# Expert stage of a fused attention and mixture kernel: its buffers laid into the feed-forward's tiles, and its first gathers written earlier

## The chip, the cores and the metric

The kernel runs on one core of a Trainium2 chip. The metric is the device time of one execution in microseconds (us). Several executions are timed and their median is given; one further execution is recorded by the hardware profiler, and all rows below come from that one.

A core has a matrix engine (TensorE, PE in the rows; PEld is its loading of weights), a vector engine (VectorE, DVE), a scalar engine (ScalarE, ACT), a general engine (GpSimd, POOL) and SyncE (SP). Each works through a queue of its own in order and waits for the others by semaphores. SP and POOL also issue DMAs; PSUM is the memory into which TensorE writes.

## The reference

Three layers follow each other, on 2304 tokens of width 512:

```
attn = softmax(causal(q k^T / 8 + decay)) v       # 4 batches, 8 heads, 576 tokens
h    = attn @ w_in;  x = (h * clip(h + 3, 0, 6) / 6) @ w_out       # inner width 2048
e    = argmax(x @ w_gate)                          # one of 8 experts for each token
out  = prob(e) * sigmoid(x @ w_output_gate)[e] * (relu(x @ w1[e]) @ w2[e])   # inner width 1024
```

The change concerns the last layer, the expert stage, and the end of the layer in front of it.

## The kernel before

Numbers are kept as pairs of 16-bit values, a high part in f16 and a low part in bf16, so a product takes three matmuls (high x high, high x low, low x high). `P` is 128, `KD` is 4 (512 / 128), `E` is 8, `F2` is 1024, `CT` is 384.

The feed-forward runs over six chunks of 384 tokens (`moe1_steps`). Its weights lie in `wi` and `wo` in SBUF, its inner values in `g` (also seen as the flat `gf`; `wof` is the flat `wo`), its input chunks in two tiles with the tag `xT`. These tiles belong to pools `mp` and `mpi`, which the context `moe1_ctx` holds. `gate_steps` works out expert, rank and weight of each token and writes the chunk's result, row by row, into a DRAM tile `rows`.

An expert's tokens are found by their rank in it. `table` builds, by matmuls with one-hot tiles `R`, the token numbers (`ids`) and weights (`cf`) for slots of 128 tokens, called blocks: block 0, 1 and 2 of each expert. `gather` then issues for each block an indirect DMA from POOL, which fetches 128 rows of `rows` into `xg` (256 KB), and a transposing DMA from SP, which turns them into `xs`. `expert1` is the first product: 8 steps, each 12 matmuls into one PSUM tile, then a relu on ACT that writes the high part of `hT` and a subtraction on DVE that writes the low part. `expert2` is the second product, 24 matmuls for a block; ACT weighs the result into `y`, and an indirect DMA from POOL scatters it to the output.

Blocks 0 of experts 0 and 1 hold tokens of the chunks that are done first. They are gathered and computed early, around the last chunk's gating, with the lists `first` and a room in `wi` for everything. Then the expert stage proper (`round_`) goes through experts 0 to 7: first product of the main blocks (`main[e]`: block 1 for experts 0 and 1, blocks 0 and 1 for the others), block 2 under a branch that is taken only where the expert has more than 256 tokens (its two products are the third block), and the second product of the main blocks. In this data experts 0, 1, 4 and 6 take the branch.

The experts' weights come as f32, 512 KB at a time, by DMA from SP into a stage tile (`fetch` inside `weights_steps`), and are split into high part (ACT) and low part (DVE) in `W1` and `W2`, two tiles each. An expert has eight such parts. Experts 0 and 1 are split during the last chunk; `spread` hands out the other 48 splits between the steps of the products. Stage tiles are three in the pool `wp`, and four in the pool `xp` once `round_` starts. `xp` is opened behind the early blocks, after `moe1_ctx` is closed, and so takes the room of `wi`, `wo`, `g` and the chunks:

```
    moe1_ctx.close()
    xp = ctx.enter_context(tc.tile_pool(name="xp", bufs=1))
    stw_in[:] = xp, 4
```

`xg` has three tiles there, `xs` and `hT` two, `y` three. For TensorE, ACT and DVE the order in the expert stage is that in which the code is written (`manual_schedule`); for POOL and SP the scheduler sets it at build time.

Of the kernel before, what the change touches and what calls it, by code (L numbers as in the profile page):

```python
# [7 lines left out]
F16 = mybir.dt.float16  # L8
# [10 lines left out]
P = 128  # L19
# [39 lines left out]
def attention_moe_kernel(ctx: ExitStack, tc: tile.TileContext, q, k, v, f, w_in, w_out,  # L59
# [781 lines left out]

    stw_in, fetches = [], []

    def weights_steps(wp):

        parts, tiles = [], {}

        def add(e, which):  # L850
            wv = (w1, w2)[which][e].rearrange("(k p) f -> p k f", p=P)
            for i in range(KD):
                n = F2 // P // KD
                parts.append((wv[:, i] if which == 0 else wv[:, n * i:n * i + n], e, which,
                              i if which == 0 else slice(n * i, n * i + n)))

        for e, which in ((0, 0), (1, 0), (0, 1), (1, 1)):
            add(e, which)
        for e in range(2, E):
            add(e, 0)  # L860
            add(e, 1)
        sts = []

        def fetch():
            pool, bufs = stw_in
            st = pool.tile([P, F2], F32, tag="stw", name="stw", bufs=bufs)
            src = parts[len(sts)][0]
            if len(src.shape) == 3:
                st = st.rearrange("p (a b) -> p a b", a=src.shape[1])
            nc.sync.dma_start(out=st, in_=src)  # L870
            sts.append(st)

        for _ in range(3):
            fetch()
        fetches.append(fetch)
        yield
        for i, (_, e, which, js) in enumerate(parts):
# [68 lines left out]
    def gather(e, pool, blocks, into=None):  # L946

        n = len(blocks)
# [12 lines left out]
    def h_tile(e, blocks, into=None):  # L961
        n = len(blocks)
# [26 lines left out]
    def expert2(e, pool, ps_pool, blocks, into=None):  # L989

        W2 = wts[e, 1]
        NF2 = F2 // P
        for s in blocks:
            hT, ho = h_t[e, s]
            ps = ps_pool.tile([P, 512], F32, tag="mm", name="mm")
            i = 0
            for m in range(NF2):
                for a, b2 in ((0, 0), (0, 1), (1, 0)):
                    l, r = hT[:, m, a, ho:ho + P], W2[:, b2, m, :]
                    nc.tensor.matmul(ps, lhsT=l.bitcast(BF16) if a else l, rhs=r.bitcast(BF16) if b2 else r,  # L1000
                                     start=i == 0, stop=i == 3 * NF2 - 1)
# [71 lines left out]
    def open_weights():  # L1073
        nonlocal wp, wg_
        while adv():
            pass
        attn_ctx.close()
        wp = ctx.enter_context(tc.tile_pool(name="wp", bufs=1, side="right"))
        stw_in[:] = wp, 3
        wg_ = weights_steps(wp)  # L1080

    for c in range(NCH):
# [13 lines left out]
        for _ in moe1_steps(c):  # L1096
# [29 lines left out]
            if c == NCH - 1 and k_ > 8:  # L1126
                for i in [rq.pop(0) for _ in range(min(2, len(rq)))]:
                    rank_onehot(R0, i, 0, P)
                    rank_onehot(R, i, P, CAP)
                    if i == NBL - 1:  # L1130
                        reserve()
                        table(R0, 0, const, ps_mm, (0,), NBL)
                        for e in range(2):
                            row = wi[:, 0, 2 * e]
                            gather(e, None, (0,), (row[:, 0:2 * DM].rearrange("p (a b) -> p a b", b=P),
                                                   row[:, 2 * DM:4 * DM]))
                            h_tile(e, (0,), wi[:, 0, 2 * e + 1].rearrange("p (a c b) -> p a c b", c=2, b=P))
        if c < NCH - 1:
# [18 lines left out]
    run(first[0], 3)  # L1157
    run(first[1], 2)
    table(R, P, const, ps_mm, (1, 2), NB)
    for g_ in first:  # L1160
        run(g_, F2 // P)
    regs = []
    for e in range(2):
        for _ in expert2(e, None, ps_mm, (0,), wi[:, 1, e, 0:2 * DM].bitcast(F32)):
            pass
        if e == 0:
            regs.extend(nc.values_load(cnt[0:1, x:x + 1], min_val=0, max_val=NT) for x in range(E))  # L1167
            more = nc.values_load(nrounds[0:1, 0:1], min_val=0, max_val=NT // CAP)  # L1168
    moe1_ctx.close()
    xp = ctx.enter_context(tc.tile_pool(name="xp", bufs=1))  # L1170
    stw_in[:] = xp, 4

    def round_(first):
        main = [(1,) if first and e < 2 else (0, 1) for e in range(E)]

        def fetch(e):
            blocks = main[e] + (2,)
            gather(e, xp, blocks)
            h_tile(e, blocks)

        def when(e):

            return tc.If(regs[e] > CAP - P) if first else nullcontext()

        def spread(g, n):

            done = 0
            for i, _ in enumerate(g):
                if done < n and i % 2 == 0:
                    run(wg)  # L1190
                    done += 1
            run(wg, n - done)

        def first_product(e):
            spread(expert1(e, ps2, main[e]), KD if 0 < e < E - 1 else 0)
            with when(e):  # L1196
                for _ in expert1(e, ps_mm, (2,)):
                    pass
                for _ in expert2(e, xp, ps_mm, (2,)):
                    pass  # L1200

        wg = wg_
        if not first:
            wg = weights_steps(wp)
            run(wg, 4 * KD + 1)
        fetch(0)
        fetch(1)
        for _ in range(2 if first else 0):
            fetches[0]()
        for e in range(E):  # L1210
            first_product(e)
            if e + 2 < E:
                fetch(e + 2)
            spread(expert2(e, xp, ps2, main[e]), KD if e + 2 < E else 0)

    round_(True)
    manual.close()
    with tc.If(more > 0):
        RA = xp.tile([P, NB, CAP], F16, name="RA")
        with tc.For_i(0, more, 1):  # L1220
            nc.vector.tensor_scalar(out=rank, in0=rank, scalar1=-float(CAP), scalar2=None, op0=ALU.add)
            for i in range(NB):
                rank_onehot(RA, i, 0, CAP)
            table(RA, 0, xp, ps_mm, range(NSB), NB)
            round_(False)


# [28 lines left out]
```

## Time and profile before

| | us |
|---|---|
| median of 3 timed runs | 832.36 |
| lowest and highest of them | 831.86, 833.91 |
| the profiled execution | 829.8 |
| its span, first to last instruction | 828.1 |
| TensorE busy in the span | 738.6 (89%) |
| VectorE, ScalarE, GpSimd busy | 466.0, 450.5, 314.8 |

Attention and feed-forward overlap until about 550 us; the early blocks follow the last chunk at 581, and the expert stage fills the rest. Shares over the whole span say little about one stage, so stretches are read by windows and timelines. A time in a row is counted from the first instruction.

### The profile page before, as it was taken

How to read it: one execution, taken by the hardware profiler on the slowest of the kernel's cores; microseconds unless marked ns; L12 is line 12 of the kernel's file. 1: busy time of each engine (PE TensorE's matmuls, PEld its weight loads, DVE VectorE, ACT ScalarE, POOL GpSimd, SP SyncE). 2: the span in 40 equal slices, each digit the busy share in tenths (PEclk: the TensorE clock that was granted, in tenths of full speed). 3: DMA queues.
4: the chain of work that ended last, by engine and by line, in shares of the span. 5: the costliest groups of instructions: out<-in, count | busy, mean ns of one | idle time of the engine just before them, and what ended most of it. 6: DMA issues, size and time to landing. Idle time of an engine off the chain costs nothing. (4 is left out here: it accounts for less than half of the span.)

```text
span 828.1 us, 16598 instructions
## 1 busy us (share of the span) xinstructions
PE 738.6 (89%) x6177; PEld 477.7 (58%) x6177; DVE 466.0 (56%) x1267; ACT 450.5 (54%) x909; POOL 314.8 (38%) x393
## 2 busy tenths in 40 slices
PE   4756988988899999999999999999929899999994
PEld 2543555645566655566555656666707666756761
DVE  8998997547632855168515785740502566535410
ACT  4865789767973684479525665530203465535420
POOL 9557788755762453256413400000022132220010
PEclk9976989989999999999999999999969999999997
DMA  9767899979994783578515567420356599979010
GB/s 248 234 184 181 185 226 246 186 126 175 173 179 104 142 141 62 92 146 152 82 36 124 102 222 234 123 49 4 78 183 123 164 301 309 293 196 279 31 38 28
DMA packets 263778, 127.95 MB, mean 155 GB/s; under 512 B 214658, under 2 KB 247522, under 8 KB 263684
## 3 DMA queue, kind: packets, MB, share of 16 engines
q1 hardware_dynamic: 251860, 105.20, 57.8%
q0 software_dynamic: 4960, 15.73, 5.4%
q10 hardware_dynamic: 6864, 5.80, 2.6%
q8 instruction: 54, 0.88, 0.4%
q14 instruction: 40, 0.33, 0.1%
HBM read 71.52 MB, written 10.08 MB: 99 GB/s over the span
## 5 line engine op out<-in xcount | busy, mean ns | idle before, releaser
L695 PE MATMUL mm<-xT,wi 128*128 128x384 f16 (+1 forms) x1152 | 211.4, 331 | 7.9 <-DMA xT<-xn 5.2
L718 PE MATMUL mm<-g,wo 128*128 128x384 f16 (+1 forms) x1152 | 198.3, 326 | 1.5 <-DVE hr L702 1.4
L695 PEld LDWEIGHTS <-wi 128*128 128x128 f16 (+1 forms) x1152 | 111.2, 99 | 83.7 <-issue 15.6
L718 PEld LDWEIGHTS <-wo 128*128 128x128 f16 (+1 forms) x1152 | 111.0, 98 | 74.6 <-issue 3.6
L981 PEld LDWEIGHTS <-W 128*128 128x128 f16 (+1 forms) x1344 | 101.1, 99 | 28.2 <-issue 20.0
L981 PE MATMUL mm<-xs,W 128*128 128x256 f16 (+3 forms) x1152 | 98.2, 248 | 19.2 <-DMA xs<-xg 16.4
L884 DVE TENSOR_TENSOR W<-stw,W 128x1024 bf16<-128x1024 f32 x64 | 77.3, 1224 | 58.3 <-ACT W L883 57.7
L394 POOL TENSOR_TENSOR pn<-ms,pn 128x384 bf16<-128x384 f32 (+1 forms) x80 | 83.1, 1044 | 57.8 <-ACT pn L393 53.9
L376 ACT ACTIVATE ms<-ms,nm 128x512 f32<-128x512 f32 (+4 forms) x144 | 79.4, 576 | 37.6 <-DVE nm L342 26.4
L1000 PE MATMUL mm<-W,hT 128*128 128x512 f16 (+1 forms) x432 | 94.7, 379 | 1.1 <-ACT W L883 0.5
L883 ACT ACTIVATE W<-stw 128x1024 f16<-128x1024 f32 x64 | 66.3, 1052 | 21.6 <-DMA stw<-in_moe_w_dram 21.2
L985 DVE SCALAR_TENSOR_TENSOR hT<-mm,hT 128x128 bf16<-128x128 f32 (+1 forms) x96 | 33.0, 355 | 74.7 <-ACT hT L984 72.5
L342 DVE CUSTOM_DVE_ANT_1 ms<-sc,mask 128x128 f32<-128x128 f32 (+3 forms) x128 | 59.1, 485 | 24.8 <-PE sc L295 13.9
L707 DVE TENSOR_TENSOR g<-hr,g 128x384 bf16<-128x384 f32 x80 | 54.4, 682 | 31.2 <-ACT g L703 31.0
L1000 PEld LDWEIGHTS <-hT 128*128 128x128 f16 (+1 forms) x432 | 41.8, 98 | 51.3 <-ACT W L883 1.2
L702 DVE SCALAR_TENSOR_TENSOR hr<-hr,mm 128x384 f32<-128x384 f32 x96 | 52.7, 549 | 28.2 <-ACT hr L699 27.4
L699 ACT ACTIVATE hr<-mm,bias 128x384 f32<-128x384 f32 x96 | 54.5, 568 | 18.3 <-PE mm L695 16.2
L1007 POOL DMA_INDIRECT out_dram<-y,ids x18 | 18.7, 1038 | 119.0 <-ACT y L1006 102.4
L703 ACT ACTIVATE g<-hr 128x384 f16<-128x384 f32 x96 | 49.3, 516 | 26.4 <-DVE hr L702 25.8
L984 ACT ACTIVATE hT<-mm 128x128 f16<-128x128 f32 (+1 forms) x96 | 31.1, 331 | 53.9 <-PE mm L981 53.8
L428 PE MATMUL pv<-vt,pt 128*128 128x65 f16 x320 | 42.4, 199 | 17.0 <-DVE xs L453 8.6
L295 PE MATMUL sc<-K,q 128*128 128x256 f16 (+3 forms) x192 | 49.2, 297 | 7.0 <-DVE nm L342 6.8
(189 smaller groups left out, 1122.0 us busy)
## 6 DMA issues: line engine op xcount, KB each, us to landing
stw<-in_moe_w_dram SPq DMA_DIRECT2D x64, 512.0 KB
wo<-in_moe_w_in_dram SPq DMA_DIRECT2D x16, 512.0 KB
raw<-in_moe_w_out_dram ACTq DMA_DIRECT2D x11, 512.0 KB
rows<-rw POOLq DMA_DIRECT2D x15, 256.0 KB, 2.8
ldk<-in_k_dram SPq DMA_DIRECT2D x14, 256.0 KB
ldq<-in_q_dram SPq DMA_DIRECT2D x14, 256.0 KB
ldv<-in_v_dram SPq DMA_DIRECT2D x13, 256.0 KB
g<-in_moe_w_out_dram SPq DMA_DIRECT2D x3, 512.0 KB
```

The costliest lines, as they stand in the source:

```text
L342: nc.vector.tensor_tensor_reduce(out=pairs(ms[:, off:off + w]), in0=ps[:, 0:w].rearrange("p (c j) -> p c j", c=2), in1=pairs(mask[:, 640 - ...
L376: nc.scalar.activation(out=ms[:, off:off + w], in_=ms[:, off:off + w], func=AF.Exp, scale=-1.0, bias=nm[:, i:i + 1])
L394: nc.gpsimd.tensor_tensor(out=lo.bitcast(BF16), in0=ms[:, 0:N], in1=hi, op=ALU.subtract)
L695: nc.tensor.matmul(ps[:, 0:w], lhsT=l.bitcast(BF16) if a else l, rhs=r.bitcast(BF16) if b2 else r, start=i == 0, stop=i == 3 * KD - 1)
L699: nc.scalar.activation(out=hr, in_=ps[:, 0:w], func=AF.Relu, bias=bias3)
L702: nc.vector.scalar_tensor_tensor(out=hr, in0=hr, scalar=6.0, in1=ps[:, 0:w], op0=ALU.min, op1=ALU.mult)
L707: either.tensor_tensor(out=g[:, m, 1, 0:w].bitcast(BF16), in0=hr, in1=g[:, m, 0, 0:w], op=ALU.subtract)
L718: nc.tensor.matmul(ps[:, 0:w], lhsT=l.bitcast(BF16) if a else l, rhs=r.bitcast(BF16) if b2 else r, start=i == 0, stop=i == 3 * NF - 1)
L883: nc.scalar.activation(out=hi, in_=sts[i], func=AF.Copy)
L884: nc.vector.tensor_tensor(out=lo.bitcast(BF16), in0=sts[i], in1=hi, op=ALU.subtract)
L981: nc.tensor.matmul(ps[:, 0:w], lhsT=l.bitcast(BF16) if a else l, rhs=r.bitcast(BF16) if b2 else r, start=i == 0, stop=i == 3 * KD - 1)
L1000: nc.tensor.matmul(ps, lhsT=l.bitcast(BF16) if a else l, rhs=r.bitcast(BF16) if b2 else r, start=i == 0, stop=i == 3 * NF2 - 1)
```

## The change

Everything that lay in `xp` now lies in the feed-forward's own tiles, and `moe1_ctx` stays open: `xs` takes two rooms and `xg` six rooms in `g`, `hT` takes two rooms and `y` four rooms in `wo`. The rooms of `xg` and `y` are handed out by `row_tile`, whose one count `taken` serves both. Stage tiles are a ring of five: the three of `wp` and two of the chunks' `xT` tiles (named `stx`). Gathers of the first two experts, and two weight fetches, are written in front of the rest of the early blocks' code. `spread` takes the number of steps and gives expert 1's first product two splits instead of four, and expert 6's second product two instead of none.

```
-            st = pool.tile([P, F2], F32, tag="stw", name="stw", bufs=bufs)
+            if ring:
+                st = ring.pop(0)
+                ring.append(st)
+            else:
+                st = wp.tile([P, F2], F32, tag="stw", name="stw", bufs=3)
+                made.append(st)
...
+    taken = [0]
+
+    def row_tile(room):
+
+        i = taken[0] % (room.shape[1] // (2 * DM))
+        taken[0] += 1
+        return room[:, i * 2 * DM:(i + 1) * 2 * DM]
...
-            xs = pool.tile([P, 2 * KD, NSB * P], F16, tag="xs2", name="xs2", bufs=2)[:, :, 0:n * P]
-            xg = [pool.tile([P, 2 * DM], F16, tag="xg", name="xg", bufs=3) for _ in blocks]
+            n = 2 * KD * NSB * P
+            xs = gf[:, e % 2 * n:(e % 2 + 1) * n].rearrange("p (a b) -> p a b", a=2 * KD)
+            xg = [row_tile(gf[:, 2 * n:]) for _ in blocks]
...
-            into = xp.tile([P, F2 // P, 2, NSB * P], F16, tag="hT", name="hT", bufs=2)
+            n = F2 // P * 2 * NSB * P
+            into = wof[:, e % 2 * n:(e % 2 + 1) * n].rearrange("p (a c b) -> p a c b", c=2, b=NSB * P)
...
-            y = pool.tile([P, DM], F32, tag="y", name="y", bufs=3) if into is None else into
+            y = row_tile(wof[:, 4 * F2 // P * NSB * P:]).bitcast(F32) if into is None else into
...
+    for e in range(2):
+        fetch(e, main[e] + (2,))
+    extra = [mp.tile([P, 2 * KD, CT], F16, tag="xT", name="stx", bufs=2) for _ in range(2)]
+    ring.extend(t.rearrange("p a b -> p (a b)")[:, 0:2 * F2].bitcast(F32) for t in extra)
+    ring.extend(made[-3:])
+    for _ in extra:
+        fetches[0]()
     for g_ in first:
         run(g_, F2 // P)
...
-    moe1_ctx.close()
-    xp = ctx.enter_context(tc.tile_pool(name="xp", bufs=1))
-    stw_in[:] = xp, 4
...
-            spread(expert1(e, ps2, main[e]), KD if 0 < e < E - 1 else 0)
...
+            n1 = 0 if e in (0, E - 1) else KD // 2 if e == 1 else KD
+            n2 = KD if e < E - 2 else KD // 2 if e == E - 2 else 0
+            spread(expert1(e, ps2, blocks[e]), F2 // P, n1)
...
-            spread(expert2(e, xp, ps2, main[e]), KD if e + 2 < E else 0)
+            spread(expert2(e, ps2, blocks[e]), F2 // P // 2 * len(blocks[e]), n2)
```

Lines move by the change: `gather`'s indirect DMA and transpose stand at L955 and L958 before and at L967 and L970 after, the weight load at L870 and L874, the scatter at L1007 and L1019, the split's copy at L883 and L887, the relu that writes `hT` at L984 and L996, the weighing into `y` at L1006 and L1018.

POOL's queue behind the last write of `rows`, before (`wi` as a source of the scatter is the early blocks' result):

```order
L793 DMA rows<-wi 128x1024 x3
L1007 DMA out_dram<-wi,ids 2304x512 x2
L955 DMA xg<-rows,ids 128x1024 x7
L1167 TENSOR_LOAD cnt
L1196 COMPARE_AND_BRANCH
L1007 DMA out_dram<-y,ids 2304x512
```

The same place of the change, from the third write on, each with the semaphores that it waits for (DMASW: a DMA issued by POOL, DMAHW: one issued by SP):

```order
L793 DMA rows<-wi 128x1024 [waits DMAHW2_49]
L967 DMA g<-rows,ids 128x1024 [waits DMASW2_49,DMASW1_49,DMASW3_49,DVE_49,PE_49]
L967 DMA g<-rows,ids 128x1024
L967 DMA g<-rows,ids 128x1024 [waits DVE_49]
L967 DMA g<-rows,ids 128x1024 [waits DMASW7_49]
L967 DMA g<-rows,ids 128x1024 [waits DMASW0_49]
L967 DMA g<-rows,ids 128x1024
L967 DMA g<-rows,ids 128x1024 [waits DMAHW3_49,DMASW6_49]
L967 DMA g<-rows,ids 128x1024 [waits DMAHW4_49,DMASW7_49]
L1019 DMA out_dram<-wi,ids 2304x512 [waits DMASW4_49,Activation_49]
```

Eight gathers now stand in front of the first early scatter, where both scatters stood in front of the gathers. The first of the eight waits for the three writes of `rows` (DMASW1 to 3). The first two are those of block 0 of experts 2 and 3, whose `ids` come from the early table and whose rooms are free; the third to sixth are those of experts 0 and 1.

SP's queue behind the last of the register loads that the branches need, before:

```order
L1168 ISA x2
L870 DMA stw<-in_moe_w_dram 128x1024
L870 DMA stw<-in_moe_w_dram 128x2x512 x3
L958 DMA_TRANSPOSE xs_8587<-xg 128x8x128 x2
L958 DMA_TRANSPOSE xs_8595<-xg 128x8x128 x2
L1196 COMPARE_AND_BRANCH
```

The same place of the change, with the waits:

```order
L970 DMA_TRANSPOSE g<-g 128x8x128 [waits DMAHW3_49,DMASW6_49,PE_49]
L970 DMA_TRANSPOSE g<-g 128x8x128 [waits DMAHW4_49,DMASW7_49]
L970 DMA_TRANSPOSE g<-g 128x8x128 [waits DMAHW5_49,DMASW0_49,PE_49]
L970 DMA_TRANSPOSE g<-g 128x8x128 [waits DMAHW6_49,DMASW1_49]
L970 DMA_TRANSPOSE g<-g 128x8x128 [waits DMAHW7_49,DMASW3_49]
L970 DMA_TRANSPOSE g<-g 128x8x128 [waits DMAHW0_49,DMAHW3_49,DMASW4_49,PE_49]
L1218 COMPARE_AND_BRANCH
L970 DMA_TRANSPOSE g<-g 128x8x128 [waits DMAHW1_49,DMAHW4_49,DMASW2_49,PE_49]
L874 DMA stw<-in_moe_w_dram 128x2x512 [waits DMAHW2_49,DVE_49]
```

The four weight loads in front of the transposes are gone from this place; two of them stand further ahead, in front of the transposes of the early blocks. The first transpose waits for the third gather of the list above (DMASW6), expert 0's. The sixth and seventh are expert 2's and wait for TensorE to be through with expert 0, and the next loads stand behind them.

ACT's queue from expert 0's third block to expert 1's branch, before and after:

```order
L1006 ACTIVATE y<-mm,cf 128x512
L1196 UNCONDITIONAL_BRANCH x2
L883 ACTIVATE W_8896<-stw 128x1024 x2
L1006 ACTIVATE y<-mm,cf 128x512
L883 ACTIVATE W_8896<-stw 128x1024 x2
L984 ACTIVATE hT<-mm 128x128
L883 ACTIVATE W_8951<-stw 128x1024
L984 ACTIVATE hT<-mm 128x128 x2
L883 ACTIVATE W_8951<-stw 128x1024
```

```order
L1018 ACTIVATE wo<-mm,cf 128x512
L1218 UNCONDITIONAL_BRANCH x2
L887 ACTIVATE W_8876<-stw 128x1024 x3
L1018 ACTIVATE wo<-mm,cf 128x512
L887 ACTIVATE W_8876<-stx 128x1024
L996 ACTIVATE wo<-mm 128x128
L887 ACTIVATE W_8926<-stx 128x1024
L996 ACTIVATE wo<-mm 128x128 x4
L887 ACTIVATE W_8926<-stw 128x1024
L996 ACTIVATE wo<-mm 128x128 x3
```

Three splits instead of two now stand in front of expert 0's main `y`, one instead of two behind it, and two instead of four between the `hT` parts of expert 1. TensorE's own queue is the same instruction for instruction but for the names.

## Rows read from the trace of the kernel before

**Rows 1.** The page's 40 slices: TensorE's busy tenths.

```profile
PE   4756988988899999999999999999929899999994
```

**Rows 2.** Windows: start and end, length, busy us (instructions) by engine, granted clock, DMA.

```profile
600.00:610.00 10.00, 5.20 (x25) 2.15 (x22) 0.00 (x0) 1.38 (x2) 2.02 (x2) 0.87 0.14 52
610.00:620.00 10.00, 0.00 (x0) 0.00 (x0) 0.00 (x0) 0.00 (x0) 2.93 (x3) 0.50 0.97 302
620.00:630.00 10.00, 8.37 (x127) 8.40 (x128) 2.63 (x9) 2.67 (x10) 2.83 (x3) 0.78 0.76 172
...
660.00:720.00 60.00, 59.21 (x408) 39.57 (x407) 34.72 (x44) 34.17 (x51) 16.89 (x15) 1.00 1.04 303
```

**Rows 3.** Timeline of PE: start, length, instruction, count, idle before and its releaser.

```profile
594.67 10.53 PE L1000 MATMUL mm<-W,wi 128*128 128x512 f16 x48
621.63 12.19 PE L981 MATMUL mm<-xs,W 128*128 128x128 f16 x192 [16.43 <-DMA xs<-xg]
...
649.83 3.51 PE L981 MATMUL mm<-xs,W 128*128 128x128 f16 x60 [0.50 <-DVE hT L985]
...
668.32 10.64 PE L981 MATMUL mm<-xs,W 128*128 128x256 f16 x96
...
806.07 10.52 PE L1000 MATMUL mm<-W,hT 128*128 128x512 f16 x48
```

**Rows 4.** Waits of PE and ACT, 621 to 820: total, times, longest.

```profile
PE mm L981 <- DVE hT L985: 2.7, 3, 1.3
PE mm L1000 <- ACT W L883: 0.5, 1, 0.5
...
ACT W L883 <- DMA stw<-in_moe_w_dram: 6.3, 6, 2.0
```

**Rows 5.** Timeline of POOL.

```profile
591.08 0.54 POOL L793 DMA_DIRECT2D rows<-wi  x1 [3.12 <-DMA wi<-x]
...
610.02 0.99 POOL L955 DMA_INDIRECT xg<-rows,ids  x1 [2.82 <-issue]
611.32 0.98 POOL L955 DMA_INDIRECT xg<-rows,ids  x1 [0.30 <-issue]
...
640.00 1.02 POOL L1007 DMA_INDIRECT out_dram<-y,ids  x1 [7.44 <-ACT y L1006]
641.32 1.45 POOL L955 DMA_INDIRECT xg<-rows,ids  x1 [0.30 <-issue]
```

**Rows 6.** SP: one wait, its timeline, and its loads from 600 to 720.

```profile
SPq L870 <- DMA out_dram<-wi,ids: 13.8, 1, 13.8
...
609.35 1.84 SPq L870 DMA_DIRECT2D stw<-in_moe_w_dram  x4
617.24 21.26 SPq L958 DMA_TRANSPOSE xs<-xg  x7
648.27 3.20 SPq L870 DMA_DIRECT2D stw<-in_moe_w_dram  x3
...
L870 SPq DMA_DIRECT2D stw<-in_moe_w_dram x31: 328/368/579, 609.4 to 718.0; - x31
```

**Rows 7.** The early blocks' gathers at 552 (L955, 549 to 600).

```profile
L955 POOL DMA_INDIRECT wi<-rows,ids x2: 979/1014/1050, 551.8 to 553.2; - x2
...
DMA to landing us min/median/max: 3.5/3.5/3.5
```

**Rows 8.** The last chunk's writes of `rows` (L793, 580 to 600).

```profile
DMA to landing us min/median/max: 4.3/4.7/5.1
```

**Rows 9.** The gathers into `xg`.

```profile
DMA to landing us min/median/max: 3.3/5.5/7.8
```

**Rows 10.** Timelines of DVE and ACT around expert 1's first product.

```profile
640.70 2.36 DVE L884 TENSOR_TENSOR W<-stw,W 128x1024 bf16<-128x1024 f32 x2 [6.24 <-ACT W L883]
645.88 2.36 DVE L884 TENSOR_TENSOR W<-stw,W 128x1024 bf16<-128x1024 f32 x2 [2.82 <-ACT W L883]
...
644.21 0.69 ACT L1006 ACTIVATE y<-mm,cf 128x512 f32<-128x512 f32 x1 [2.60 <-PE mm L1000]
```

**Rows 11.** The scatters (L1007).

```profile
DMA to landing us min/median/max: 2.2/3.8/6.9
```

More of the change, by code (lines that the diff above doesn't have):

```diff
@@ L840, in gate_steps @@
         yield
-    stw_in, fetches = [], []
+    ring, made, fetches = [], [], []
     def weights_steps(wp):
@@ L864, in fetch @@
         def fetch():
-            pool, bufs = stw_in
-            st = pool.tile([P, F2], F32, tag="stw", name="stw", bufs=bufs)
+            if ring:
[4 more added lines that the diff above has]
+                made.append(st)
             src = parts[len(sts)][0]
@@ L944, in rank_onehot, with gather @@
                                 op0=ALU.is_equal)
-    def gather(e, pool, blocks, into=None):
-        n = len(blocks)
+    taken = [0]
[3 more added lines that the diff above has]
+        return room[:, i * 2 * DM:(i + 1) * 2 * DM]
+    def gather(e, blocks, into=None):
         if into is None:
-            xs = pool.tile([P, 2 * KD, NSB * P], F16, tag="xs2", name="xs2", bufs=2)[:, :, 0:n * P]
-            xg = [pool.tile([P, 2 * DM], F16, tag="xg", name="xg", bufs=3) for _ in blocks]
+            n = 2 * KD * NSB * P
+            xs = gf[:, e % 2 * n:(e % 2 + 1) * n].rearrange("p (a b) -> p a b", a=2 * KD)
+            xg = [row_tile(gf[:, 2 * n:]) for _ in blocks]
         else:
@@ L961, in h_tile @@
     def h_tile(e, blocks, into=None):
-        n = len(blocks)
         if into is None:
-            into = xp.tile([P, F2 // P, 2, NSB * P], F16, tag="hT", name="hT", bufs=2)
+            n = F2 // P * 2 * NSB * P
+            into = wof[:, e % 2 * n:(e % 2 + 1) * n].rearrange("p (a c b) -> p a c b", c=2, b=NSB * P)
         for j, s in enumerate(blocks):
@@ L987, in expert1, with expert2 @@
             yield
-    def expert2(e, pool, ps_pool, blocks, into=None):
+    def expert2(e, ps_pool, blocks, into=None):
         W2 = wts[e, 1]
@@ L1078, in open_weights @@
         wp = ctx.enter_context(tc.tile_pool(name="wp", bufs=1, side="right"))
-        stw_in[:] = wp, 3
         wg_ = weights_steps(wp)
@@ L1134, in attention_moe_kernel @@
                             row = wi[:, 0, 2 * e]
-                            gather(e, None, (0,), (row[:, 0:2 * DM].rearrange("p (a b) -> p a b", b=P),
+                            gather(e, (0,), (row[:, 0:2 * DM].rearrange("p (a b) -> p a b", b=P),
                                                    row[:, 2 * DM:4 * DM]))
@@ L1159, in attention_moe_kernel, with fetch @@
     table(R, P, const, ps_mm, (1, 2), NB)
+    regs = []
+    main = [(1,) if e < 2 else (0, 1) for e in range(E)]
+    def fetch(e, blocks):
+        gather(e, blocks)
+        h_tile(e, blocks)
+    for e in range(2):
[5 more added lines that the diff above has]
+        fetches[0]()
     for g_ in first:
         run(g_, F2 // P)
-    regs = []
     for e in range(2):
-        for _ in expert2(e, None, ps_mm, (0,), wi[:, 1, e, 0:2 * DM].bitcast(F32)):
+        for _ in expert2(e, ps_mm, (0,), wi[:, 1, e, 0:2 * DM].bitcast(F32)):
             pass
@@ L1168, in attention_moe_kernel, with spread @@
             more = nc.values_load(nrounds[0:1, 0:1], min_val=0, max_val=NT // CAP)
-    moe1_ctx.close()
-    xp = ctx.enter_context(tc.tile_pool(name="xp", bufs=1))
-    stw_in[:] = xp, 4
     def round_(first):
[L1174 to L1179, printed above, removed]
         def when(e):
             return tc.If(regs[e] > CAP - P) if first else nullcontext()
-        def spread(g, n):
-            done = 0
+        def spread(g, steps, n):
             for i, _ in enumerate(g):
-                if done < n and i % 2 == 0:
+                if n and i % (steps // n) == 0 and i // (steps // n) < n:
                     run(wg)
-                    done += 1
-            run(wg, n - done)
-        def first_product(e):
-            spread(expert1(e, ps2, main[e]), KD if 0 < e < E - 1 else 0)
+        wg = wg_
+        blocks = main
+        if not first:
+            blocks = [(0, 1)] * E
+            wg = weights_steps(wp)
+            run(wg, 4 * KD + 1)
+            for e in range(2):
+                fetch(e, (0, 1, 2))
+        for e in range(E):
+            n1 = 0 if e in (0, E - 1) else KD // 2 if e == 1 else KD
+            n2 = KD if e < E - 2 else KD // 2 if e == E - 2 else 0
+            spread(expert1(e, ps2, blocks[e]), F2 // P, n1)
             with when(e):
@@ L1198, in first_product @@
                     pass
-                for _ in expert2(e, xp, ps_mm, (2,)):
+                for _ in expert2(e, ps_mm, (2,)):
                     pass
[L1202 to L1211, printed above, removed]
             if e + 2 < E:
-                fetch(e + 2)
-            spread(expert2(e, xp, ps2, main[e]), KD if e + 2 < E else 0)
+                fetch(e + 2, (0, 1, 2))
+            spread(expert2(e, ps2, blocks[e]), F2 // P // 2 * len(blocks[e]), n2)
     round_(True)
@@ L1218, in attention_moe_kernel @@
     with tc.If(more > 0):
-        RA = xp.tile([P, NB, CAP], F16, name="RA")
+        RA = wi.rearrange("p a b c -> p (a b c)")[:, 0:NB * CAP].rearrange("p (n s) -> p n s", s=CAP)
         with tc.For_i(0, more, 1):
@@ L1223, in attention_moe_kernel @@
                 rank_onehot(RA, i, 0, CAP)
-            table(RA, 0, xp, ps_mm, range(NSB), NB)
+            table(RA, 0, mp2, ps_mm, range(NSB), NB)
             round_(False)
```

## Prediction

> **What bounds the kernel now.** I first read the page's 40 slices of 20.7 us [rows 1]: TensorE shows 9 tenths in nearly every slice from the second quarter on, with one hole, a 2 in the slice of 600 to 621. Windows of 10 us show it closer [rows 2]: TensorE is busy 5.20 us in 600-610 and not at all in 610-620, and its granted clock reads 0.87, 0.50 and 0.78 of 2.4 GHz in the three windows from 600, so it fell to the 1.2 GHz level in the pause and came back only behind it. TensorE's timeline [rows 3] names both sides: the 48 matmuls of the early blocks' second product end at 594.67 + 10.53 = 605.20, and the 192 of expert 0's first product begin at 621.63, after 16.43 us of waiting for the DMA into `xs`. From there TensorE runs to 806.07 + 10.52 = 816.59, and its list of waits for that stretch [rows 4] has 2.7 us behind the `hT` parts of expert 1's first product (three pauses) and 0.5 us behind a split, no more.
>
> So from 605.2 to 816.6 it is TensorE's own work behind one long wait. What makes up that wait is read from the queues. GpSimd issues the first gather of the expert stage at 610.02 [rows 5]. On SP [rows 6] four weight loads start at 609.35, in front of the transposes, and SP had waited 13.8 us for a scatter that reads `wi` before it could issue the first: the new pool lay in that room. The transposes begin at 617.24, and TensorE starts 4.39 us later. The gather thus took 617.24 - 610.02 = 7.2 us to be usable, against 3.5 us for the same operation at 552 with little traffic [rows 7].
>
> **The change, part by part.**
>
> *No new pool, gathers in front.* Nothing that the gathers, transposes and loads write now lies in `wi`. The first gather still needs the last write of `rows`, issued at 591.08 [rows 5]. Such a write lands 4.3 to 5.1 us after its issue [rows 8], so GpSimd can issue gathers from 595.4 (4.3 taken, since the third write is alone). By the order in the change section, experts 2's and 3's first gathers come ahead of expert 0's: two places at 1.30 us (610.02 to 611.32), so expert 0's first gather is issued at 598.0. It lands after 3.5 us [rows 7], since no weight load is under way then, at 601.5, and from transpose to TensorE it is 4.39 us: 605.9. TensorE is free at 605.2, so 0.7 us of the 16.43 remain: **15.7 us gained**. From both sides: with the fastest landing of any gather, 3.3 us [rows 9], the pause is 0.5 us, and a transpose that has the DMA engines to itself may well take it to nothing, 16.4 gained; with 5.1 us for the write and the median 5.5 for the gather [rows 9] the data are there at 608.7 and 12.9 are gained. I stay near the upper end because the gather at 552 is the same operation in the same quiet.
>
> The Trainium skill's page "DMA: Bandwidth & Descriptors", section on the anatomy of one DMA, fits a DMA issued by GpSimd as about 2.0 us plus its bytes at 436 GB/s, which for 256 KB makes an estimate of 2.6 us. The row has 3.5 us for that size. By the page the sum would be 0.7 us better, with no pause left at all.
>
> *The clock.* Expert 0's 192 first-product matmuls took 12.19 us; 60 of the same line and shape took 3.51 us a little later [rows 3], so 192 take 11.23 us at the 2.4 GHz level. Without a long pause ahead of them the clock should not have fallen: **0.95 us gained**, nothing if the pause stays long.
>
> *Fewer splits by expert 1.* A split is a ScalarE copy and a VectorE subtraction of some 1.2 us (two in 2.36 [rows 10]). Before, two splits of the previous step (645.88) and four more stand between the `hT` parts of expert 1's first product in VectorE's queue, and TensorE waits for those parts, since they free its PSUM tiles. Two of the four are gone: 2.4 us less in that queue, against 2.7 us of pauses. I leave 0.8 us, because the split at step 4 still stands ahead of the last three parts: **1.9 us gained**, bounds 0.5 and 2.7. The two splits turn up at the other end, in expert 6's second product: 2.4 us of VectorE beside 10.5 us of matmuls, which hide them as long as their loads are there; without that cover expert 7's second product would wait for them.
>
> *A shared count of row tiles.* Four rooms for `y` are more than three, but the count `taken` runs on over gathers and outputs alike, so the room of expert 0's third block is also that of its main block (counts 4 and 8, both 0 modulo 4; experts 1 and 4 alike). ScalarE must hold the main block's `y` until the third block's scatter has landed. Before, that scatter was issued at 640.00 [rows 5] and the main block's `y` began at 644.21 [rows 10], so it has 4.2 us. A scatter takes 2.2 to 6.9, median 3.8 [rows 11]: a wait of 0 to 2.7 us, which holds up the `hT` parts queued behind it on ScalarE. **0.3 us lost** taken.
>
> *The ring of stage tiles.* Five tiles throughout replace seven that shrink to four. Each later load waits for the split five places back, not four. The two extra loads are issued around 550, when table and matmuls that read their rooms are done, and the two transposes behind them on SP feed products that start 25 us later. ScalarE waited 6.3 us in sum for loads [rows 4]. Zero, bounded by the third rival.
>
> **Sum.** 15.7 + 0.95 + 1.9 - 0.3 = 18.25 us. The profiled execution took 829.8 us (span 828.1 and 1.7 around it) and becomes 811.6. The median of the three timed runs is 832.36, 2.6 above that execution; the same gain gives **814.0** rounded. About 0.3%, 2.5 us, is what a measurement of this kernel can tell from no change.
>
> **Rivals.**
>
> *The chain is late all the same.* Eight gathers in a row on GpSimd, with transposes behind them, may land as slowly as the one at 610. If expert 0's takes 7.2 us again, TensorE starts at 598.0 + 7.2 + 4.4 = 609.6: 4.4 us of pause and perhaps the clock lost again, so 817.7 to 818.7. For it: the chain has no slack. Against it: the four loads that shared the DMA engines with the old gathers are gone. A gather also took 1.45 us to issue beside two splits on VectorE (641.32), and 0.98 with VectorE idle [rows 5, 10]; three as slow as that cost 1.4 us. The Trainium skill's page "SBUF — State Buffer" (two separate sides) warns that some VectorE operations keep GpSimd from writing descriptors. By that rule the moved gathers could stretch; the trace agrees only beside splits.
>
> *Expert 1's pauses stay.* If the wait for `y` takes its 2.7 us and the splits give 0.5, the gain is 15.7 + 0.95 + 0.5 - 2.7 = 14.45: 817.9.
>
> *The loads become the bound, and the kernel slower.* SP's queue holds transposes that wait for TensorE in front of loads. Before, 27 loads (31 but for the first four) were issued from 648.27 to 718.0, 2.7 us apart [rows 6], with the DMA share at 1.04 in 660-720 [rows 2]. The eight loads of an expert make 21.4 us at that pace, and TensorE's work for an expert without a third block 10.64 + 10.52 = 21.2 us [rows 3]. So the loads have nothing to spare there. 43 of them remain when the first tile comes free, at about 625. At 2.7 us each they are through at 741, far ahead of expert 7's second product at some 788. It decides from (788 - 625) / 43 = 3.8 us a load, and to be slower than before by 2.5 us takes 4.3 us: 835 or more.
>
> *The change doesn't take.* If another wait keeps expert 0's first product at 621, only the split and `y` terms are left: 830.8. That product waits for its transpose alone besides its engine's order, so I give this little.
>
> **Chances.** The sum as forecast 0.64 (its own range 811.5 to 816.5); late chain 0.17; expert 1's pauses 0.11; loads that bind a little (819 to 829) 0.03 and to a loss 0.03; no effect 0.02. The range 811.0 to 820.0 holds the first three but for their tails. Faster 0.95, same 0.02, slower 0.03.
>
> **What would show it.** Right: a pause of TensorE at 605 under 2 us and a granted clock of 1.00 in 600-630; gathers on GpSimd from 595 and SP's first transpose near 601; pauses in expert 1's first product under 1.5 us in sum; TensorE at work until about 798. Wrong: a transpose issued past 603, `y` of expert 0's main block starting well behind its last matmul, or ScalarE waiting for loads with TensorE idle behind it.

## The result, and the profile after

The changed kernel takes 811.27 us (median of 4, 811.10 to 814.34), the kernel before in the same comparison 832.11 (median of 4, 830.28 to 833.91): a ratio of 0.9758, interval 0.9727 to 0.9790. The forecast was 814.0, with a range of 811 to 820; the measured time is at its lower edge, and just below the 811.5 to 816.5 that the forecast gave its own sum. The profiled execution of the changed kernel is the slowest of its four, 814.34 us with a span of 812.6.

That execution was late already ahead of the change. The early blocks' second product ends at 605.20 us before [rows 3] and at 608.73 now, and in the ten profiled executions of the experiments this end lies between 606.6 and 611.8. So I compare one **stage**, from the end of that product to the end of the last matmul: 816.59 - 605.20 = 211.39 us before, 800.94 - 608.73 = 192.21 now. The stage became **19.18 us** shorter; the forecast sum was 18.25.

TensorE's line of the page, which answers [rows 1], has lost its hole:

```profile
PE   4755988989899999998999999999999999999994
```

Windows of the changed kernel, columns as in [rows 2]:

```profile
600.00:610.00 10.00, 8.73 (x41) 3.85 (x40) 0.00 (x0) 1.38 (x2) 3.79 (x4) 1.00 0.87 188
610.00:620.00 10.00, 9.54 (x171) 9.54 (x171) 3.79 (x13) 3.61 (x13) 4.54 (x5) 1.00 0.84 201
620.00:630.00 10.00, 10.00 (x66) 5.17 (x63) 2.65 (x5) 4.27 (x7) 2.53 (x3) 1.00 0.40 77
660.00:720.00 60.00, 59.70 (x461) 40.71 (x459) 33.23 (x50) 32.28 (x53) 13.36 (x12) 1.00 0.94 269
```

TensorE is busy 8.73 and 9.54 us where it was busy 5.20 and 0.00, and its granted clock stays at 1.00 where [rows 2] has 0.87, 0.50 and 0.78. TensorE's timeline, and its waits from 608 to the end:

```profile
598.21 10.52 PE L1012 MATMUL mm<-W,wi 128*128 128x512 f16 x48
610.46 10.88 PE L993 MATMUL mm<-g,W 128*128 128x128 f16 x192 [1.73 <-DMA g<-g]
621.18 10.52 PE L1012 MATMUL mm<-W,wo 128*128 128x512 f16 x48
631.54 4.22 PE L993 MATMUL mm<-g,W 128*128 128x128 f16 x72
636.27 6.86 PE L993 MATMUL mm<-g,W 128*128 128x128 f16 x120 [0.50 <-DVE wo L997]
...
790.42 10.52 PE L1012 MATMUL mm<-W,wo 128*128 128x512 f16 x48
```

```profile
PE mm L993 <- DMA g<-g: 1.7, 1, 1.7
PE mm L993 <- DVE wo L997: 0.5, 1, 0.5
```

The names have moved: `g` holds what was `xs` and `xg`, `wo` what was `hT` and `y`. Against [rows 3, 4]: the first pause is 1.73 us for 16.43 (14.70 gained), the first 192 matmuls take 10.88 for 12.19 (1.31), expert 1's pauses are 0.50 in sum for 2.75 (2.25), and the 0.5 us behind a split is gone. That is 18.8 of the 19.18; the rest I can't place.

The chain that sets the first pause, on GpSimd and SP:

```profile
594.61 0.54 POOL L793 DMA_DIRECT2D rows<-wi  x1 [3.03 <-DMA wi<-x]
597.68 0.99 POOL L967 DMA_INDIRECT g<-rows,ids  x1 [2.53 <-DVE wi L997]
...
600.27 0.95 POOL L967 DMA_INDIRECT g<-rows,ids  x1 [0.30 <-issue]
```

```profile
604.02 19.50 SPq L970 DMA_TRANSPOSE g<-g  x7
```

The gather at 597.68 begins 3.07 us after the last write of `rows`; the profile gives a VectorE instruction as its releaser, but what it needs is that write: in four of the experiments' executions the distance is 3.07 or 3.08 us again, while the releaser named is another. Expert 0's gather is the third, at 600.27. Its transpose starts 3.75 us later, at 604.02, and TensorE 6.44 us after that.

### The profile page after: what moved, and what is told of

Same layout as the page of the kernel before. It is cut to its first block, busy times and chain, and to the rows that moved or that the text cites. A ratio compares the mean times of both kernels' runs of the same rounds, so it can differ in the third digit from the quotient of the medians.

```text
span 812.6 us, 16609 instructions
## 1 busy us (share of the span) xinstructions
PE 738.5 (91%) x6177; PEld 477.0 (59%) x6177; DVE 464.6 (57%) x1267; ACT 451.3 (56%) x909; POOL 317.8 (39%) x393
## 5 line engine op out<-in xcount | busy, mean ns | idle before, releaser
L718 PEld LDWEIGHTS <-wo 128*128 128x128 f16 (+1 forms) x1152 | 111.0, 98 | 75.0 <-issue 4.0
L993 PE MATMUL mm<-g,W 128*128 128x256 f16 (+3 forms) x1152 | 96.6, 246 | 2.2 <-DMA g<-g 1.7
L1012 PE MATMUL mm<-W,wo 128*128 128x512 f16 (+1 forms) x432 | 94.5, 379 | 0.6
L888 DVE TENSOR_TENSOR W<-stw,W 128x1024 bf16<-128x1024 f32 x46 | 55.6, 1222 | 53.3 <-ACT W L887 53.1
L1012 PEld LDWEIGHTS <-wo 128*128 128x128 f16 (+1 forms) x432 | 41.8, 98 | 50.8 <-ACT W L887 1.2
L1019 POOL DMA_INDIRECT out_dram<-wo,ids x18 | 19.5, 1082 | 118.8 <-ACT wo L1018 97.6
L997 DVE SCALAR_TENSOR_TENSOR wo<-mm,wo 128x128 bf16<-128x128 f32 (+1 forms) x96 | 33.2, 355 | 48.9 <-ACT wo L996 46.4
L887 ACT ACTIVATE W<-stw 128x1024 f16<-128x1024 f32 x46 | 47.6, 1050 | 15.0 <-DMA stw<-in_moe_w_dram 14.9
L996 ACT ACTIVATE wo<-mm 128x128 f16<-128x128 f32 (+1 forms) x96 | 31.5, 331 | 41.4 <-PE mm L993 35.8
```

Source lines behind the costliest of these rows:

```text
L718: nc.tensor.matmul(ps[:, 0:w], lhsT=l.bitcast(BF16) if a else l, rhs=r.bitcast(BF16) if b2 else r, start=i == 0, stop=i == 3 * NF - 1)
L993: nc.tensor.matmul(ps[:, 0:w], lhsT=l.bitcast(BF16) if a else l, rhs=r.bitcast(BF16) if b2 else r, start=i == 0, stop=i == 3 * KD - 1)
```

## The experiments

Each kernel is the changed one with the edit shown, but for one that starts from the kernel before. Times of different comparisons are not set against each other, since the kernel before itself had medians of 832 to 837 us in them; ratios and the stage are.

**The room, put back.** The gathers' room, or the four loads that went along with them? Here the loads stay away, and expert 0's gather gets a room in `wi` that an early scatter reads. Its code has to move behind the early blocks' for that; the other gathers still start at 598.57.

```diff
+            if e == 0 and len(blocks) == 2:
+                xg[0] = wi[:, 1, 1, 0:2 * DM]
...
-    for e in range(2):
-        fetch(e, main[e] + (2,))
...
+
+    for e in range(2):
+        fetch(e, main[e] + (2,))
```

> The changed kernel, but expert 0's first gather goes into the room of the second early block's result, so that it waits again for that scatter to land; no pool is opened and the weight loads stay where the change has them. If the wait for the early scatters is what cost the 16.4 us: the gather is issued 3 to 4 us behind the scatter of about 610, its data are usable 8 to 10 us later, TensorE's pause is 12 to 17 us and the time 821 to 827. Rival, that the four weight loads in front of the transposes cost most of it: the pause stays under 6 us and the time under 816.

834.56 us against 835.58, ratio 0.9976 (0.9943 to 1.0008): the whole gain is gone. Timelines of TensorE, GpSimd and SP:

```profile
599.21 10.52 PE L1014 MATMUL mm<-W,wi 128*128 128x512 f16 x47
627.94 13.50 PE L995 MATMUL mm<-g,W 128*128 128x128 f16 x192 [18.21 <-DMA g<-wi]
...
614.04 1.03 POOL L1021 DMA_INDIRECT out_dram<-wi,ids  x1 [0.31 <-issue]
618.60 0.99 POOL L1021 DMA_INDIRECT out_dram<-wi,ids  x1 [3.53 <-issue]
621.60 0.98 POOL L969 DMA_INDIRECT wi<-rows,ids  x1 [2.00 <-DMA out_dram<-wi,ids]
...
624.85 1.23 SPq L972 DMA_TRANSPOSE g<-wi  x1
```

A window of the same kernel:

```profile
615.00:630.00 15.00, 2.06 (x20) 2.06 (x20) 0.28 (x1) 0.28 (x1) 2.05 (x3) 0.50 0.39 99
```

The gather at 621.60 waits for the scatter's landing; transpose and product follow at once. The pause is 18.21 us, above what was expected, because the scatters themselves came late: they stand behind gathers on GpSimd that wait for transposes, and for the second one's last 3.53 us the profile names no releaser. It was issued 8.87 us behind the early blocks' product (609.73), and before the change 1.00 us behind it (605.20):

```profile
606.20 1.00 POOL L1007 DMA_INDIRECT out_dram<-wi,ids  x1 [4.17 <-ACT wi L1006]
```

So the pause is as long as the old one but made up differently. Here it takes 11.87 us to the gather's issue, and 6.34 from there to TensorE; in [rows 3, 5] it was 4.82 and 11.61. With the scatter as early as before the pause would be some 18.21 - 7.87 = 10.3 us, an estimate. The wait for the room is shown and is the larger part, so the rival on the loads (under 6 us) fell. That the full 16.4 us came back is a coincidence: about 5 us of the old pause (11.61 - 6.34) lie in a gather and a transpose that had the four loads beside them, and those loads had waited for the same room. The clock is at its 1.2 GHz level (0.50) in 615 to 630, and the 192 matmuls take 13.50 us.

**The splits, each way.** First the changed kernel with four splits by expert 1, as before, then the kernel before with the new counts, then the changed kernel with the new counts placed by the old rule.

```diff
-            n1 = 0 if e in (0, E - 1) else KD // 2 if e == 1 else KD
-            n2 = KD if e < E - 2 else KD // 2 if e == E - 2 else 0
+            n1 = 0 if e in (0, E - 1) else KD
+            n2 = KD if e < E - 2 else 0
```

> The changed kernel with four splits again in expert 1's first product and none in expert 6's second. If those splits made the pauses there: pauses of 2.0 to 2.75 us in expert 1's first product where the change has 0.5, and 1.5 to 2.3 us more time (813 to 813.6). Rival, that earlier loads and the deeper ring took the pauses away: no difference, 811 to 811.6.

```diff
-            spread(expert1(e, ps2, main[e]), KD if 0 < e < E - 1 else 0)
+            spread(expert1(e, ps2, main[e]), KD // 2 if e == 1 else KD if 0 < e < E - 1 else 0)
...
-            spread(expert2(e, xp, ps2, main[e]), KD if e + 2 < E else 0)
+            spread(expert2(e, xp, ps2, main[e]), KD if e + 2 < E else KD // 2 if e == E - 2 else 0)
```

> The kernel before with the new counts of splits alone (two in expert 1's first product, two in expert 6's second). If this term is independent of the rest: the pauses of 2.7 us in expert 1's first product shrink to 0.3 to 1.0 and the time falls by 1.7 to 2.4 us (about 830). Rival, that the pauses come from loads that arrive late: less than 0.7 us.

```diff
+            done = 0
...
-                if n and i % (steps // n) == 0 and i // (steps // n) < n:
+                if done < n and i % 2 == 0:
...
+                    done += 1
+            run(wg, n - done)
```

> The changed kernel with the old rule that places splits (two at the first and third step, the rest behind the last) and the new counts. The new counts alone took 1.28 us off the pauses in expert 1's first product, the change 2.25. If the rest is the third split that the new rule puts ahead of expert 0's main output: pauses of 0.97 and 0.50 us there, as in the kernel before with the new counts, and a stage of 193.2 us. Rival, that the rest comes from loads that are there sooner: 0.5 us of pauses, a stage of 192.2 us.

Pauses in expert 1's first product, from TensorE's timelines of the three in order:

```profile
612.60 12.51 PE L993 MATMUL mm<-g,W 128*128 128x128 f16 x192 [2.51 <-DMA g<-g]
...
640.03 3.51 PE L993 MATMUL mm<-g,W 128*128 128x128 f16 x60 [0.50 <-DVE wo L997]
644.82 3.51 PE L993 MATMUL mm<-g,W 128*128 128x128 f16 x60 [1.28 <-DVE wo L997]
```

```profile
651.93 0.83 PE L981 MATMUL mm<-xs,W 128*128 128x128 f16 x12 [0.97 <-DVE hT L985]
653.27 6.86 PE L981 MATMUL mm<-xs,W 128*128 128x128 f16 x120 [0.50 <-DVE hT L985]
```

```profile
609.63 5.58 PE L993 MATMUL mm<-g,W 128*128 128x128 f16 x68 [2.49 <-DMA g<-g]
...
638.45 0.83 PE L993 MATMUL mm<-g,W 128*128 128x128 f16 x12 [1.01 <-DVE wo L997]
639.78 6.86 PE L993 MATMUL mm<-g,W 128*128 128x128 f16 x120 [0.50 <-DVE wo L997]
```

Four splits under the new rule leave 1.78 us of pauses, two under the old rule 1.51 in the changed kernel and 1.47 (0.97 + 0.50) in the kernel before, two under the new rule 0.50, and four under the old rule 2.75. The 1.78 and the 1.47 fall between what the two theories expected, since neither had a part for the placing; the 1.51 is as expected. So fewer splits are worth 1.28 us by themselves under either rule, and the placing about 1.0: three splits of the previous step stand ahead of expert 0's main `y` in the changed kernel, two in [rows 10], so one less stands between the `hT` parts. The run times don't resolve this: ratios of 0.9761 (0.9681 to 0.9841) for the first and 0.9990 (0.9964 to 1.0015) for the second, 817.89 us in one run for the third. The stages of the first and third, 196.06 and 197.37 us, are longer than the splits make them: their first pauses were 2.51 and 2.49 us, and the granted clock read 0.83 in 610-620 and 0.66 in 610-615 behind them.

**Rooms of row tiles.** Is the chain's lateness the two gathers ahead of expert 0's, and does a shared count of four rooms make `y` wait?

```diff
-            xg = [row_tile(gf[:, 2 * n:]) for _ in blocks]
+            xg = [row_tile(gf[:, 2 * n:2 * n + 4 * 2 * DM]) for _ in blocks]
```

> The changed kernel with four rooms for gathered rows instead of six, so that the first gathers of experts 2 and 3 find no free room and come behind those of experts 0 and 1. If those two places on GpSimd make the 1.7 us that is left of the pause: expert 0's gather is issued 2.6 us earlier, the pause goes to 0.0 to 0.3 us, and the time falls by 1.4 to 1.7 us (about 809.6). Rival, that the transpose is slow because the next gathers share the DMA engines with it: 0.8 us or more of the pause stays.

818.20 us, ratio 0.9744 (0.9682 to 0.9805), stage 198.07. Expert 0's gather is first in the queue now, and its product starts without a pause. But expert 1's has two new ones; TensorE's rows, ScalarE's list of waits for 600 to 700, a window of 3 us, and the third block's scatter:

```profile
635.71 0.83 PE L993 MATMUL mm<-g,W 128*128 128x128 f16 x12 [3.85 <-ACT wo L1018]
638.11 10.24 PE L993 MATMUL mm<-g,W 128*128 128x128 f16 x132 [1.57 <-DVE wo L997]
```

```profile
ACT wo L1018 <- DMA out_dram<-wo,ids: 7.4, 1, 7.4
...
639.00:642.00 3.00, 3.00 (x31) 2.94 (x29) 2.52 (x8) 0.88 (x3) 0.00 (x0) 0.50 0.82 258
...
DMA to landing us min/median/max: 6.8/6.8/6.8
```

ScalarE waits 7.4 us to write the main block's `y`, for the scatter of the third block's out of the same room, and the `hT` parts queue behind it. This is the wait that the prediction described. The change has the same shared room, but there that scatter landed in 2.3 us, and here in 6.8. Behind the pause of 3.85 us the granted clock fell to 0.50, and the 132 matmuls took 10.24 us, where the pace of 120 in 6.86 makes 7.5. With a count of its own for `y` it should be gone:

```diff
-    taken = [0]
+    taken = [0, 0]
...
-    def row_tile(room):
+    def row_tile(room, of=0):
...
-        i = taken[0] % (room.shape[1] // (2 * DM))
-        taken[0] += 1
+        i = taken[of] % (room.shape[1] // (2 * DM))
+        taken[of] += 1
...
-            y = row_tile(wof[:, 4 * F2 // P * NSB * P:]).bitcast(F32) if into is None else into
+            y = row_tile(wof[:, 4 * F2 // P * NSB * P:], 1).bitcast(F32) if into is None else into
```

> The changed kernel with four gather rooms and a count of its own for the rooms of the outputs. With four rooms alone the pause at the head was gone, but expert 0's main output waited 7.4 us for the room that the third block's scatter still read, and TensorE lost 5.4 us in expert 1's first product. If the shared count is the cause: no pause at the head (under 0.3 us), pauses in expert 1's first product back at 0.5 or less, and from the end of the early blocks to the last matmul 190.2 to 190.8 us against 192.2 of the change. Rival, that the gathers held on GpSimd for transposes are the cause: 2 us or more stay in expert 1's first product.

817.22 us, ratio 0.9804 (0.9773 to 0.9835), stage 192.91. ScalarE's wait and the first pause are gone, and expert 1's pause is 0.49 again: without the shared count there is no such wait. TensorE stalled 1.27 us in three pauses that the profile calls issue at 611 to 613, and 0.73 more at the next product, so nothing was won in this execution. To see whether this version beats the change, both ran on one chip:

> The changed kernel as it stands, beside the next run on the same chip. Every theory: 811 to 815 us, a ratio to the kernel before of 0.974 to 0.980; stage from the end of the early blocks' second product to the last matmul 192 to 196 us, a first pause of 1.7 to 2.5 us and one pause of 0.5 us in expert 1's first product.

> Four rooms for the first gathers, with a count of their own for y, beside the changed kernel on the same chip. If the first pause of 1.7 us is what is left of the old wait and nothing takes its place, this is 1.5 to 2.5 us faster than the changed kernel (ratio lower by 0.002 to 0.003). If the short stalls of TensorE that the profile calls issue come back at 611 to 616 us, as in the earlier run of it (1.3 us in all, and 0.7 us at the next wait), the two are within 1 us of each other, stage 192 to 194 us in both.

814.79 us, ratio 0.9766 (0.9727 to 0.9805), for the change; 815.68, ratio 0.9752 (0.9721 to 0.9782), for the other. TensorE's timeline, first of the change, then of the other:

```profile
608.34 10.88 PE L993 MATMUL mm<-g,W 128*128 128x128 f16 x192 [1.74 <-DMA g<-g]
```

```profile
606.50 5.34 PE L1012 MATMUL mm<-W,wi 128*128 128x512 f16 x24 [0.31 <-issue]
611.68 10.88 PE L993 MATMUL mm<-g,W 128*128 128x128 f16 x192
```

The stalls did not come back, and the stage is 190.27 us against 192.44: 2.2 less, the first pause and a little. The medians and the intervals don't show it, and the two executions of the second kernel differ by 2.6 (192.91 and 190.27). In its execution here the early blocks ended 5.2 us later than in that of the change, whether by chance or by the other order of gathers stays open. I don't call it a faster kernel.

**Traffic beside the gathers.** Four loads that nobody uses, beside the moved gathers, put back what the old place had.

```diff
+    for x, (i, j) in enumerate(((0, 0), (0, 2), (1, 2), (1, 3))):
+        nc.scalar.dma_start(out=wi[:, i, j].bitcast(F32), in_=w1[E - 1][x * P:(x + 1) * P])
```

> The changed kernel with four weight loads of 512 KB more, which nothing reads, issued by ScalarE when the early blocks' first products are through (some 598), so that they share the DMA engines with the first gathers as the four old loads did. If traffic beside them is what made a gather take 7.2 us before: expert 0's gather, usable 3.75 us after its issue in the change, takes 5.5 to 7.5 us, its transpose longer too, and the pause grows from 1.7 to between 4 and 7 us. Rival, that the gathers and transposes are slow by themselves: the pause stays under 2.7 us.

818.38 us in one run, stage 197.68. Timelines of TensorE and SP, and then windows of 5 us:

```profile
612.10 7.28 PE L993 MATMUL mm<-g,W 128*128 128x128 f16 x102 [4.90 <-DMA g<-g]
...
606.32 21.13 SPq L970 DMA_TRANSPOSE g<-g  x7
```

```profile
605.00:610.00 5.00, 2.20 (x11) 0.88 (x9) 0.00 (x0) 0.88 (x2) 0.00 (x0) 1.00 1.20 307
610.00:615.00 5.00, 2.90 (x28) 2.90 (x28) 0.29 (x1) 0.41 (x2) 1.90 (x2) 0.67 0.97 188
```

Expert 0's gather, issued at 598.32, needs 8.0 us to the transpose for 3.75, a little more than expected, and the first pause is 4.90 us. Such loads would have made the late chain of the first rival.

**The ring of stage tiles.** The ring without its two extra tiles and the loads into them: three in place of five.

```diff
-    extra = [mp.tile([P, 2 * KD, CT], F16, tag="xT", name="stx", bufs=2) for _ in range(2)]
-    ring.extend(t.rearrange("p a b -> p (a b)")[:, 0:2 * F2].bitcast(F32) for t in extra)
...
-    for _ in extra:
-        fetches[0]()
```

> The changed kernel with a ring of three stage tiles, without the two of the chunks' room and without the two early fetches. If the loads have slack as the forecast took it: ScalarE waits longer for loads (10 to 25 us in sum), TensorE loses under 2 us by it, and the stage from the early blocks' end to the last matmul takes 192 to 194.5 us. Rival, that the loads are close to being the bound: 197 us or more.

823.11 us in one run, stage 202.05. One row of ScalarE's list of waits from 600 on, two of TensorE's, and a row of its timeline:

```profile
ACT W L887 <- DMA stw<-in_moe_w_dram: 33.1, 22, 3.7
...
PE mm L993 <- DVE wo L997: 5.4, 4, 2.4
...
PE mm L1012 <- ACT W L887: 1.4, 1, 1.4
```

```profile
640.50 6.86 PE L993 MATMUL mm<-g,W 128*128 128x128 f16 x120 [2.42 <-DVE wo L997]
```

ScalarE waits 33.1 us for loads, where the change has no such row from 600 on, and TensorE loses up to 2.42 us at a time behind the late splits, four times. That is more than I expected, and the rival held: the loads lie closer to the bound than taken. The two extra tiles with their early loads are worth 6 to 8 us of stage. It is 9.8 longer, of which 1.8 are stalls that the profile calls issue; 6.3 are waits behind splits (5.4 and 1.4, for 0.5 in the change).

## Why the prediction was right, step by step

*The pool's wait.* Right in mechanism and nearly in size: 14.70 us for 15.7. The first experiment shows the mechanism, since a gather that waits for the room starts late again and the gain is gone; the old pause was that wait and the slower gather and transpose behind it. Set against [rows 3, 5], 13.28 us of the 14.70 come from the earlier issue (4.82 us behind the early blocks' product before, 8.46 ahead of it now) and only 1.42 from a faster gather and transpose (10.19 us for 11.61); the forecast had 12.0 and 3.7. Two terms of the chain were mis-sized, against each other. The last write of `rows` was taken at 4.3 us, the least of [rows 8]; the landing of that very write, and of expert 0's gather, read now:

```profile
DMA to landing us min/median/max: 2.3/2.3/2.3
...
DMA to landing us min/median/max: 3.7/3.7/3.7
```

The write landed in 2.3 us and the gather behind it was issued at 3.07; expert 0's gather in 3.7, for 3.5 taken. The two places ahead cost 2.59, as taken. That the early write and the late transpose nearly cancel is luck. **From transpose to TensorE it was 6.44 us, not 4.39.** I had taken [rows 6] as the slow end, with four loads under way, and thought a transpose with the engines to itself faster. It isn't by itself: the gathers behind it, up to 604.02, and the other transposes share the DMA engines, whose share is 0.87 in 600-610. A single transpose late in the first experiment took 627.94 - 624.85 = 3.09 us, at a DMA share of 0.39. That the sharing makes the difference fits these rows, but no experiment took the later gathers away alone, and the share by itself doesn't order them: the 4.39 us before had a share of 1.16 in 617.24-621.60. Nor is 6.44 a fixed price: it was 6.32 in the other execution of the change (602.02 to 608.34) and 7.58 with four splits (605.02 to 612.60), which have the same order here.

The Trainium skill's page "DMA: Bandwidth & Descriptors" gave an estimate of 2.6 us for the gather and no pause left. The rows have 3.7 to usable data and a pause of 1.73, so the row at 552 was the better guide than the page's fit.

*GpSimd's issue.* The six moved gathers, and all 22 of the stage:

```profile
L967 POOL DMA_INDIRECT g<-rows,ids x6: 947/947/991, 597.7 to 604.0; - x6
```

```profile
L967 POOL DMA_INDIRECT g<-rows,ids x22: 942/978/1939, 597.7 to 724.4; - x22
```

None of the moved ones took over 1 us to issue; the slow ones stand beside splits, up to 1.94. So the rival of stretched gathers fell. The Trainium skill's page "SBUF — State Buffer" (two separate sides) gives its warning for VectorE's 2-port modes; no row shows the mode of the splits' subtractions, so whether they slowed the issue by that rule stays open.

*The clock.* 1.31 us for 0.95: the matmuls took 10.88, less than the 11.23 scaled from 60 of them.

*The splits.* 2.25 us for 1.9, within the bounds. The prediction counted only how many; the runs give 1.28 to the number and about 1.0 to the new places.

*The shared count.* 0 for -0.3. ScalarE's row for expert 0's main `y`:

```profile
631.79 0.69 ACT L1018 ACTIVATE wo<-mm,cf 128x512 f32<-128x512 f32 x1 [1.71 <-PE mm L1012]
```

It waits for its own matmul alone. The third block's scatter, issued at 627.53, landed in 2.3 us, the low end of [rows 11]. The wait is real when that scatter lands late: 7.4 us with four gather rooms, beyond the 2.7 that the prediction gave as its most.

*The loads.* They hold, at zero cost. Those from 629.5 on:

```profile
L874 SPq DMA_DIRECT2D stw<-in_moe_w_dram x27: 328/368/530, 629.5 to 752.3; - x27
L874 SPq DMA_DIRECT2D stx<-in_moe_w_dram x16: 340/380/1032, 640.2 to 744.1; - x16
```

43 loads in 752.3 - 629.5 = 122.8 us are 2.9 us each, below the 3.8 at which they would decide; 43 was the forecast's count, and it had them through at 741. But zero stood on the ring of five, which I had treated as neutral; three tiles cost 6 to 8 us.

*The signs.* The prediction named a transpose past 603 as a sign of being wrong, and the first starts at 604.02. It gave absolute times, and this execution is 3.5 us late at the early blocks' end; against that end the transpose comes 4.7 us ahead, for 3.7 by the forecast (605.2 - 601.5). Gathers from 597.68 and the last matmul's end at 800.94 are, with the 3.5 us taken off, at 594.2 and 797.4, for 595 and 798.

*The total.* The stage gained 19.18 us for 18.25, for the 1.0 that the first pause fell short is made up by clock, splits and count (0.36, 0.35 and 0.3), and 0.9 more had no term: the 0.5 behind a split, and 0.4 that I can't place. The medians gained 20.84. The remaining 1.7 us lie within the shift of the part ahead of the stage from one execution to the next, but no row shows them.

## What to carry to other kernels

A pause ahead of a stage is read backwards through its queues to the instruction that is late first, and then to what that instruction may not overwrite: here most of 16.4 us of idle TensorE were the price of a room, directly and through the loads that waited for it too, and giving the data another room took 14.7 of them away. A moved chain is no faster than its new neighbours let it be: count what else it puts on the DMA engines, since four loads beside a gather made 3.75 us into 8.0. Rooms in rotation tie together whatever shares a count, so a change of one count can make another tile wait, once the transfer it is tied to lands late.

## What the hardware showed unexpectedly

The clock behind short pauses: behind first pauses of 1.73, 1.74 and 2.23 us the granted clock stayed at 1.00, as it did behind one of 2.42 us later on with three stage tiles. Behind 2.49 and 2.51 us it fell (0.66 in 610-615 and 0.83 in 610-620), and behind 3.85 and 4.90 us too (0.50 in 639-642 and 0.67 in 610-615). The product that followed the 2.51 took 12.51 us for 10.88; with four splits:

```profile
610.00:620.00 10.00, 7.49 (x105) 7.40 (x104) 2.04 (x7) 2.85 (x9) 3.89 (x4) 0.83 0.89 189
```

Pauses that differ by 0.3 us thus stood ahead of products that differ by 1.6; whether the length of the pause decides it, these few executions don't settle.

TensorE stalled for 0.4 to 1.0 us at a time without a releaser ("issue") at 611 to 616 us in three of the executions (with a count of its own, with three stage tiles, with the old placing), for 0.21 and 0.35 us at 619 to 620 with the idle loads, and not in the second execution of the very kernel with a count of its own. The DMA share was 0.8 to 1.1 there, and 0.81 in 610-615 in the execution without them; what the stalls are stays open.

One kernel's early blocks ended at 608.69 and at 611.84 us in two profiled executions, so a stage's own length told more than the whole time, where intervals of the ratio are 0.5 to 1.6% wide. Even a stage differed by 2.6 us between those two, 2.0 of it by the stalls and the wait behind them; what a row shows by itself is a single pause with its releaser.
